# Attention into a gated feed-forward layer: both groups of a head pair multiplied by v in one visit, from the third batch on

## The chip, the cores and the metric

The kernel runs on one core of a Trainium2 chip, as one launch. The metric is the device time of one execution in microseconds (us), as the median of several runs. The core's engines each work through an instruction stream of their own in order: TensorE (PE, with its weight loads shown as PEld), VectorE (DVE), ScalarE (ACT), GpSimd (POOL) and SyncE (SP), which here issues most of the DMAs.

## The reference

Causal attention with a decay that comes from forget gates f, and a feed-forward layer on its output. Batch 8, 8 heads, 576 tokens, head size 64; so 4,608 tokens of width 512, and a hidden width of 1,536.

```python
scores = scale * np.matmul(q, k.transpose(0, 1, 3, 2))
cum = np.cumsum(np.log(np.clip(f, 0.0001, 1.0)), axis=-1)
decay = cum[:, :, :, None] - cum[:, :, None, :]
scores = np.where(causal, -1e9, scores + decay)      # causal: keys after the query
attn = softmax(scores)
x = np.matmul(attn, v)  # to (tokens, heads * head_dim)
out = (silu(x @ w_gate) * (x @ w_val)) @ w_out
```

All inputs and the output are float32; the kernel multiplies in bfloat16 and accumulates in float32.

## The kernel before

**Attention.** The work goes by pairs of heads: 8 batches of 4 pairs, 32 pairs `p`. The two heads of a pair lie side by side on the 128 partitions. Queries are cut into 9 blocks of 64 (block `i` has keys 0 to 64(i+1)), taken in the order 8, 4, 5, 6, 7, 0, 1, 2, 3. For a pair:

- q and k are loaded, made bfloat16 (POOL, from the second batch on) and transposed on PE (`transposes`, line 417) into the one PSUM bank `tt`: first k, six matmuls, copied out by ACT to `kt` (L426); then q, eight matmuls, copied out in two halves to `qz`, each by DVE or ACT (L434). `tt` has one buffer, so each of these uses waits until the copies of the one before have ended.
- for each block the scores are multiplied (L506, bank tag `sp`, two buffers), the mask is added by a second matmul (L510), DVE adds the decay and takes a minimum into `tm` (L523), ACT takes the exponential and its sum (L541), and POOL scales the rows by the reciprocal of the sum into `pk` (L564).
- the weights are transposed, so that keys lie on the partitions: from the second batch on by a DMA transpose that SP issues (`turned`, L586), into `pT1` or `pT0`, two buffers each; in the first batch on PE.
- the transposed weights are multiplied by v (`weighted`, L632), and the sums copied to `xT` by ACT (L642).

The last two steps are done in two groups of blocks, in this order: group 1 is blocks 8 to 4 (19 slots of 128 keys by one block, 10 matmuls), group 0 is blocks 3 to 0 (6 slots, 4 matmuls). A matmul of `weighted` has 64 columns of v as its weights, one head of the pair, and writes 64 partitions; the other head's writes the other 64. All other matmuls in the stretch have 128 weight columns. In the profile these forms are shown as 128*64 and 128*128. Group sums lie in the bank tag `xo`, which has one buffer, so the second group's product waits for the copy of the first one's sums.

**Feed-forward part.** Tokens are cut into 9 tiles of 512. For each, `gate` does 12 times two products with 512 columns (`gp`, `vp`, L674), a tanh on ACT (L680) and two DVE operations (L684, L690); `project` multiplies the result by `w_out` (L721), in four parts, interleaved with the next tile's gates. These products share four PSUM banks (`gv`). A gate product reads `xT` of all four pairs of its batch or batches and so waits for both groups of them. `xT` is a ring of 2,560 tokens.

**The order.** Every step is handed to the class `Planner` with an engine, a priority key (a due time), a length, what it needs, and which buffers it opens and uses. The planner plays the steps against these lengths once, before the program is built: a free engine takes the ready step with the lowest key whose buffers are free. What comes out is the fixed order of each engine's instructions. At run time an instruction waits on semaphores for its inputs and buffers, and all behind it on its engine wait too. `NPS` lists the eight PSUM banks: two for `sp`, one each for `tt` and `xo`, four for `gv`. The key of `weighted` is that of the group's scaling plus `late`, 5.0 from the second batch on; the key of the k transposes of pair `p` is five before the start of its slot (`base(p) - 5`), that of q four before.

Other readers of these steps: `ids["x", p, g]`, the product, gates the cast of v two batches later (`load_v`, which fills one of two buffers); `ids["xT", p, g]` gates the products of the feed-forward part; the DMA transpose of pair p + 2 needs the `pT` buffer that pair p's product frees.

Of the kernel before, what the change touches and what calls it, by code (L numbers as in the profile page):

```python
# [9 lines left out]
F32 = mybir.dt.float32  # L10
# [10 lines left out]
class Planner:  # L21
# [135 lines left out]
def kernel(  # L157
# [11 lines left out]
    nc = tc.nc  # L169
    B, H, S, D = q.shape  # L170
# [3 lines left out]
    P = 128  # L174
    QB = 64
    NB = S // QB
    NPB = H // 2
# [50 lines left out]
    def psum(shape, dt, name, tag):  # L228
        return ps.tile(shape, dt, name=name, tag=tag, bufs=NPS[tag])
# [4 lines left out]
    add = plan.add  # L234
# [16 lines left out]
    xT = consts.tile([P, KD, NRING], BF16)  # L251
# [14 lines left out]
    st = {}  # L266
    ids = {}
# [5 lines left out]
    def base(p):  # L273
        return 10.0 + (SLOT0 * p if p <= NPB else SLOT0 * NPB + SLOT * (p - NPB))
# [115 lines left out]
    def cast_qk(p):  # L390
# [92 lines left out]
    def scores(p):  # L483

        t0 = base(p)
# [6 lines left out]
        for i in ORDER:  # L492
# [4 lines left out]
            key = t0 + width * at / total  # L497
            at += L + 150
            for n, (a, z) in enumerate(parts):
# [13 lines left out]
                def r(i=i, a=a, z=z, n=n, last=last, L=L):  # L513
# [5 lines left out]
                    if n == 0:  # L519
# [8 lines left out]
                m = add("PE", key + 0.02 * n, 0.00042 * (z - a) + (0.03 if last else 0), s, feed,  # L528
                        opens=[("sp", p, i, a)], uses=[("kt", p)])
                ids["s", p, i] = m  # L530
                opens = [("t", p, i)] if n == 0 else []
                if i == ORDER[0] and n == 0:
                    opens.append(("sm", p))
                uses = [("sp", p, i, a), ("cb", p), ("sm", p)] + ([("t", p, i)] if n else [])
                rs = add("DVE", key + 0.3 + 0.02 * n, RED[z - a], r,
                         [m] + ([rs] if n else []), opens=opens,
                         uses=[u for u in uses if u not in opens])

            def x(i=i, L=L):
# [5 lines left out]
                                   uses=[("t", p, i), ("sm", p)])  # L545

        for i0, i1, g in SUMS:
            def rl(i0=i0, i1=i1):
                ls, rl = st["ls", p], st["rl", p]
                nc.vector.tensor_scalar(rl[:, i0:i1], ls[:, i0:i1], 1.0e-9, None, op0=ALU.add)  # L550
                nc.vector.reciprocal(rl[:, i0:i1], rl[:, i0:i1])
            kr = t0 + width * (0.82 if i0 else 1.05)
            a = add("DVE", kr, 0.3, rl, [ids["exp", p, i] for i in range(i0, i1)], uses=[("sm", p)])
            blocks = GROUPS[g]
            ns = []
            for i in sorted(blocks):
                n = blocks.index(i)
                s0 = GOFF[g] + slots_of(g, 0)[0] + n
                m = min(i // 2 + 1, 4)

                todo = [(s0, 0, m)] + ([(GOFF[g], 4, 1)] if i == 8 else [])
                for s0, c, m in todo:
                    def norm(i=i, s0=s0, c=c, m=m, w=len(blocks)):
                        nc.gpsimd.tensor_scalar(  # L564
                            pks[p % 2][:, s0:s0 + w * (m - 1) + 1:w, :],
                            evs[i][:, P * c:P * (c + m)].rearrange("p (c k) -> p c k", k=P),
                            st["rl", p][:, i:i + 1], 1.0, op0=ALU.mult, op1=ALU.mult)
                    needs = [a] + (ids["turn", p - 2, g] if p >= 2 else [])
# [44 lines left out]
    def tiles_of(a, z):  # L613
        return range(max(a, 0) // MT, (z - 1) // MT + 1) if z > 0 else ()

    def weighted(p, g, key):

        b, hp = divmod(p, NPB)
        vt = vts[b % 2]
        blocks = GROUPS[g]  # L620
        w = len(blocks)
        nch = max(blocks) // 2 + 1

        def pv():
            xo = psum([P, 5 * QB], F32, "xo", "xo")
            st["xo"] = xo
            pT = st["pT", p, g].rearrange("p s (h r) -> p s h r", h=2)
            for c in range(nch):
                s0, n = slots_of(g, c)

                for h in range(2):
                    nc.tensor.matmul(xo[64 * h:64 * h + 64, 0:n * QB], vt[:, c, 2 * hp + h, :],  # L632
                                     pT[:, s0:s0 + n, h, :],
                                     start=(c == 0), stop=(c == nch - 1))

        t0 = b * S + GTOK[g][0]

        def ev():
            tok = t0 % NRING
            assert tok + w * QB <= NRING  # L640

            nc.scalar.copy(xT[:, hp, tok:tok + w * QB].rearrange("p (s r) -> p s r", r=QB)[:, ::-1],  # L642
                           st["xo"][:, :w * QB].rearrange("p (s r) -> p s r", r=QB))
        n_slots = GLEN[g]
# [4 lines left out]
        old = [m for t in tiles_of(t0 - NRING, t0 - NRING + w * QB) for m in ids["gv", t]]  # L649
        ids["x", p, g] = a  # L650
        ids["xT", p, g] = add("ACT", key + late, 0.07 + 0.0008 * w * QB, ev, [a] + old,
                              uses=[("xo", p, g)])

# [126 lines left out]
    for b in range(B):  # L780
# [29 lines left out]
    n = KF + (NMT - 1) * (KF + NS)  # L810
# [36 lines left out]
```

## Time and profile before

| | us |
|---|---|
| median of 3 runs (lowest, highest) | 452.73 (452.68, 453.74) |
| the profiled execution's own time | 451.03 |
| its span | 449.3 |
| PE busy in the span | 406.9 (91%) |
| DVE busy | 346.6 (77%) |
| ACT busy | 302.2 (67%) |
| POOL busy | 247.1 (55%) |
| matmuls of the product with v (L632), busy | 34.6, 448 of them |
| copies of its sums to `xT` (L642), busy | 24.9, 64 of them |
| first visit of `weighted` for pair 8, for pair 31 | 126.60, 363.52 |

The profile is of one execution. Busy times of PE include a modelled end of each matmul, since matmuls overlap in the array, so the distance between two starts tells more than the printed length. A wait is put down to what ended it last. Some matmul records (a few in a hundred) are missing from the trace; weight loads are complete. "Visit" below means one run of 128*64 matmuls of `weighted` between other PE work: in the kernel before there are 64 of them, two for each pair. The last product with v ends at about 366 us; behind it come only the feed-forward part of the remaining tiles and the stores.

### The profile page before, as it was taken

How to read it: one execution, taken by the hardware profiler on the slowest of the kernel's cores; microseconds unless marked ns; L12 is line 12 of the kernel's file. 1: busy time of each engine (PE TensorE's matmuls, PEld its weight loads, DVE VectorE, ACT ScalarE, POOL GpSimd, SP SyncE). 2: the span in 40 equal slices, each digit the busy share in tenths (PEclk: the TensorE clock that was granted, in tenths of full speed). 3: DMA queues.
4: the chain of work that ended last, by engine and by line, in shares of the span. 5: the costliest groups of instructions: out<-in, count | busy, mean ns of one | idle time of the engine just before them, and what ended most of it. 6: DMA issues, size and time to landing. Idle time of an engine off the chain costs nothing.

```text
span 449.3 us, 9390 instructions
## 1 busy us (share of the span) xinstructions
PE 406.9 (91%) x2850; PEld 209.1 (47%) x2900; DVE 346.6 (77%) x1071; ACT 302.2 (67%) x838; POOL 247.1 (55%) x441
## 2 busy tenths in 40 slices
PE   1577798998799999999999999999999999999996
PEld 1355553444354554544555554554555444444442
DVE  4877779966899988988998889889989755555542
ACT  4987887745799988987878777777777532322220
POOL 2279989571978887786686777757764400000000
PEclk9998889999899999999999999999999999999999
DMA  8998979999999999999988789988882520101003
GB/s 196 230 187 174 219 153 200 172 220 215 250 221 223 212 242 203 223 224 209 220 223 188 212 217 201 218 182 204 198 138 58 129 74 23 49 24 42 30 23 117
DMA packets 156866, 75.75 MB, mean 169 GB/s; under 512 B 131600, under 2 KB 143376, under 8 KB 156816
## 3 DMA queue, kind: packets, MB, share of 16 engines
q1 hardware_dynamic: 150612, 69.70, 68.3%
q0 software_dynamic: 5808, 4.72, 8.1%
q10 hardware_dynamic: 396, 0.74, 0.6%
q8 instruction: 22, 0.36, 0.3%
q14 instruction: 28, 0.23, 0.2%
HBM read 47.33 MB, written 9.58 MB: 127 GB/s over the span
## 4 chain that ended last, share of the span: by engine, by line
PE 58%; DVE 6%; ACT 4%; issue 2%; DMA 0%; another core or an unknown queue 0%; DVEq 0%; ACTq 0%
PE op L721 17%; PE gp L674 15%; PE vp L674 14%; PE sp L506 6%; PE xo L632 4%; ACT ev L541 2%; DVE t L523 2%; PE tt L417 2%; DVE qz L434 1%; PE sp L510 1%; ACT th L680 1%; DVE ot L730 1%; DVE u L684 1%; ACT qz L434 1%; DVE hh L690 0%
## 5 line engine op out<-in xcount | busy, mean ns | idle before, releaser
L564 POOL TENSOR_SCALAR pk<-ev,rl 128x512 bf16<-128x512 f32 (+3 forms) x320 | 164.1, 533 | 94.2 <-DVE tm L523 34.6
L541 ACT ACTIVATE ev<-t,tm 128x576 f32<-128x576 f32 (+8 forms) x288 | 159.7, 556 | 25.9 <-DVE tm L523 19.0
L523 DVE CUSTOM_DVE_ANT_0 t<-sp,cb 128x512 f32<-128x512 f32 (+7 forms) x288 | 131.6, 475 | 18.5 <-PE sp L510 8.2
L674 PE MATMUL vp<-xT,wv 128*128 128x512 bf16 x413 | 121.4, 379 | 1.8 <-issue 0.6
L721 PE MATMUL op<-wo,hh 128*128 128x512 bf16 x417 | 118.9, 379 | 1.4 <-DVE u L684 0.5
L674 PE MATMUL gp<-xT,wg 128*128 128x512 bf16 x416 | 118.4, 381 | 1.4 <-DVE u L684 0.4
L506 PE MATMUL sp<-kt,qz 128*128 128x512 bf16 (+4 forms) x320 | 88.9, 298 | 17.9 <-DVE tm L523 13.8
L680 ACT ACTIVATE th<-gp 128x512 f32<-128x512 f32 x108 | 63.6, 591 | 57.7 <-PE gp L674 56.8
L684 DVE SCALAR_TENSOR_TENSOR u<-th,gp 128x512 f32<-128x512 f32 x108 | 73.4, 681 | 27.6 <-ACT th L680 27.1
L690 DVE TENSOR_TENSOR hh<-u,vp 128x512 bf16<-128x512 f32 x108 | 73.7, 682 | 12.1 <-PE vp L674 9.5
L510 PE MATMUL sp<-mask,ident 128*128 128x64 bf16 x288 | 55.6, 197 | 0.0
L721 PEld LDWEIGHTS <-hh 128*128 128x128 bf16 x432 | 37.2, 98 | 38.3 <-issue 0.8
L541 ACT ACTIVATION_READ_ACCUMULATOR ev<-t,tm 128x1 f32 x288 | 54.6, 189 | 0.0
L674 PEld LDWEIGHTS <-wg 128*128 128x128 bf16 x432 | 36.5, 98 | 35.1 <-issue 2.0
L674 PEld LDWEIGHTS <-wv 128*128 128x128 bf16 x432 | 36.1, 98 | 33.8 <-issue 1.2
L506 PEld LDWEIGHTS <-qz 128*128 128x128 bf16 x320 | 31.7, 101 | 37.5 <-issue 4.7
L510 PEld LDWEIGHTS <-ident 128*128 128x128 bf16 x288 | 28.5, 99 | 40.0 <-issue 20.5
L632 PE MATMUL xo<-pT,vt 128*64 128x320 bf16 (+4 forms) x448 | 34.6, 271 | 1.2 <-ACT xT L642 1.0
L730 DVE TENSOR_SCALAR ot<-op 128x512 f32<-128x512 f32 x27 | 18.6, 689 | 19.7 <-PE op L721 18.1
L642 ACT CAST xT<-xo 128x320 bf16<-128x320 f32 x64 | 24.9, 389 | 11.3 <-PE xo L632 11.1
L632 PEld LDWEIGHTS <-vt 128*64 128x64 bf16 x448 | 20.5, 110 | 24.9 <-issue 21.3
L401 POOL CAST kb<-kf 96x768 bf16<-96x768 f32 x30 | 25.0, 835 | 11.8 <-ACT qb L395 9.6
(52 smaller groups left out, 300.1 us busy)
## 6 DMA issues: line engine op xcount, KB each, us to landing
kf<-in_k_dram SPq DMA_DIRECT2D x32, 288.0 KB, 4.4
out_dram<-ot SPq DMA_DIRECT2D x36, 256.0 KB, 2.7
qf<-in_q_dram SPq DMA_DIRECT2D x31, 288.0 KB
cb<-cum_f SPq DMA_DIRECT2D x60, 144.0 KB, 4.3
vf<-in_v_dram SPq DMA_DIRECT2D x28, 256.0 KB, 3.3
wg<-in_moe_w_gate_dram POOLq DMA_DIRECT2D x4, 384.0 KB, 6.0
wv<-in_moe_w_val_dram POOLq DMA_DIRECT2D x4, 384.0 KB, 5.4
wo<-in_moe_w_out_dram POOLq DMA_DIRECT2D x3, 512.0 KB, 7.2
```

The source lines that it names most:

```text
L401: copy_by(nc, eng)(st["kb", p], st["kf", p].rearrange("r h c d -> r c h d"))
L506: nc.tensor.matmul(sp[:, :z - a], qz[:, i, :], st["kt", p][:, a:z], start=True, stop=not last)
L510: nc.tensor.matmul(sp[:, z - a - QB:z - a], ident, mask, start=False, stop=True)
L523: nc.vector.tensor_tensor_reduce(out=st["t", p, i][:, a:z], in0=st["sp", p, i, a][:, :z - a], in1=st["cb", p][:, a:z], scale=1.0, scalar=init,
L541: nc.scalar.activation(evs[i][:, :L], st["t", p, i][:, :L], AF.Exp, bias=tm[:, i:i + 1], scale=-1.0, accum_out=ls[:, i:i + 1])
L564: nc.gpsimd.tensor_scalar(pks[p % 2][:, s0:s0 + w * (m - 1) + 1:w, :], evs[i][:, P * c:P * (c + m)].rearrange("p (c k) -> p c k", k=P), st ...
L632: nc.tensor.matmul(xo[64 * h:64 * h + 64, 0:n * QB], vt[:, c, 2 * hp + h, :], pT[:, s0:s0 + n, h, :], start=(c == 0), stop=(c == nch - 1))
L674: nc.tensor.matmul(st[name, t, fc], w_[:, ko, fc * P:(fc + 1) * P], xT[:, ko, x0:x0 + MT], start=(ko == 0), stop=(ko == KD - 1))
L680: nc.scalar.activation(st["th", t, fc], st["gp", t, fc], AF.Tanh, scale=0.5)
L684: nc.vector.scalar_tensor_tensor(st["u", t, fc], st["th", t, fc], 1.0, st["gp", t, fc], op0=ALU.add, op1=ALU.mult)
L690: nc.vector.tensor_mul(st["hh", t][:, fc, :], st["u", t, fc], st["vp", t, fc])
L721: nc.tensor.matmul(st["op", t, s_], st["hh", t][:, fc, s_ * P:(s_ + 1) * P], wo[:, fc, :], start=(fc == 0), stop=(fc == KF - 1))
```

## The change

From pair 8 on (`APART = 2 * NPB`, the third batch) `weighted` is called once for a pair, after both groups have been scaled and their transposes planned. Its one PE step multiplies group 1 into `xo` and directly after it group 0 into a tile with the tag `tt`, the bank of the transposes of q and k. The step opens both banks, needs the transposed weights of both groups, and frees both `pT` buffers at its end. Its key is that of group 0, and its length in the plan is 0.15 plus the columns of both groups, where two steps had 0.15 each. Two copies to `xT` follow on ACT, one for each group, with the later key. Pairs 0 to 7 go as before, one group at a time through `xo`. The sums of `tt` (288 float32 columns) take as many bytes as the transposes there (576 bfloat16).

```diff
+    APART = 2 * NPB
...
             turned(p, g, GLEN[g], ns, kr)
-            weighted(p, g, kr)
+            if p < APART:
+                weighted(p, [g], kr)
+            elif g == SUMS[-1][2]:
+                weighted(p, [s[2] for s in SUMS], kr)
...
-    def weighted(p, g, key):
+    def weighted(p, gs, key):
...
+        bank = dict(zip(gs, ("xo", "tt")))
+        buf = {g: (bank[g], p, "x", g) for g in gs}
 
         def pv():
-            xo = psum([P, 5 * QB], F32, "xo", "xo")
-            st["xo"] = xo
-            pT = st["pT", p, g].rearrange("p s (h r) -> p s h r", h=2)
-            for c in range(nch):
-                s0, n = slots_of(g, c)
-
-                for h in range(2):
-                    nc.tensor.matmul(xo[64 * h:64 * h + 64, 0:n * QB], vt[:, c, 2 * hp + h, :],
-                                     pT[:, s0:s0 + n, h, :],
-                                     start=(c == 0), stop=(c == nch - 1))
...
+            for g in gs:
+                xo = psum([P, S // 2] if bank[g] == "tt" else [P, 5 * QB], F32, "xo", bank[g])
+                st["xo", p, g] = xo
+                pT = st["pT", p, g].rearrange("p s (h r) -> p s h r", h=2)
+                nch = max(GROUPS[g]) // 2 + 1
+                for c in range(nch):
+                    s0, n = slots_of(g, c)
+
+                    for h in range(2):
+                        nc.tensor.matmul(xo[64 * h:64 * h + 64, 0:n * QB], vt[:, c, 2 * hp + h, :],
+                                         pT[:, s0:s0 + n, h, :],
+                                         start=(c == 0), stop=(c == nch - 1))
+
         late = 1.5 if p < EARLY else 5.0
-        a = add("PE", key + late, 0.15 + 0.00042 * QB * n_slots, pv,
-                ids["pT", p, g] + ids["v", b], opens=[("xo", p, g)], uses=[(f"pT{g}", p)])
...
+        a = add("PE", key + late, 0.15 + 0.00042 * QB * sum(GLEN[g] for g in gs), pv,
+                [m for g in gs for m in ids["pT", p, g]] + ids["v", b],
+                opens=[buf[g] for g in gs], uses=[(f"pT{g}", p) for g in gs])
+        for g in gs:
+            w = len(GROUPS[g])
+            t0 = b * S + GTOK[g][0]
+
+            def ev(g=g, w=w, t0=t0):
...
+                nc.scalar.copy(
+                    xT[:, hp, tok:tok + w * QB].rearrange("p (s r) -> p s r", r=QB)[:, ::-1],
+                    st["xo", p, g][:, :w * QB].rearrange("p (s r) -> p s r", r=QB))
...
+            ids["x", p, g] = a
+            ids["xT", p, g] = add("ACT", key + late, 0.07 + 0.0008 * w * QB, ev, [a] + old,
+                                  uses=[buf[g]])
```

More of the change, by code (lines that the diff above doesn't have):

```diff
@@ L614, in tiles_of @@
         return range(max(a, 0) // MT, (z - 1) // MT + 1) if z > 0 else ()
-    def weighted(p, g, key):
+    def weighted(p, gs, key):
         b, hp = divmod(p, NPB)
         vt = vts[b % 2]
-        blocks = GROUPS[g]
-        w = len(blocks)
-        nch = max(blocks) // 2 + 1
+        bank = dict(zip(gs, ("xo", "tt")))
+        buf = {g: (bank[g], p, "x", g) for g in gs}
         def pv():
-            xo = psum([P, 5 * QB], F32, "xo", "xo")
-            st["xo"] = xo
-            pT = st["pT", p, g].rearrange("p s (h r) -> p s h r", h=2)
-            for c in range(nch):
-                s0, n = slots_of(g, c)
-                for h in range(2):
-                    nc.tensor.matmul(xo[64 * h:64 * h + 64, 0:n * QB], vt[:, c, 2 * hp + h, :],
-                                     pT[:, s0:s0 + n, h, :],
-                                     start=(c == 0), stop=(c == nch - 1))
[L636 to L644, printed above, removed]
-        late = 1.5 if p < EARLY else 5.0
-        a = add("PE", key + late, 0.15 + 0.00042 * QB * n_slots, pv,
-                ids["pT", p, g] + ids["v", b], opens=[("xo", p, g)], uses=[(f"pT{g}", p)])
[L649 to L652, printed above, removed]
@@ new lines, in weighted @@
+        late = 1.5 if p < EARLY else 5.0
+        a = add("PE", key + late, 0.15 + 0.00042 * QB * sum(GLEN[g] for g in gs), pv,
[5 more added lines that the diff above has]
+            def ev(g=g, w=w, t0=t0):
+                tok = t0 % NRING
+                assert tok + w * QB <= NRING
+                nc.scalar.copy(
+                    xT[:, hp, tok:tok + w * QB].rearrange("p (s r) -> p s r", r=QB)[:, ::-1],
+                    st["xo", p, g][:, :w * QB].rearrange("p (s r) -> p s r", r=QB))
+            old = [m for t in tiles_of(t0 - NRING, t0 - NRING + w * QB) for m in ids["gv", t]]
+            ids["x", p, g] = a
+            ids["xT", p, g] = add("ACT", key + late, 0.07 + 0.0008 * w * QB, ev, [a] + old,
+                                  uses=[buf[g]])
```

## The prediction

> **What bounds the kernel now.** I read the page's busy lines first, then busy time by stage, then what TensorE (PE) waits for, and last the timeline around the instructions that the change touches. In the table of stages the columns are stretch, length, then busy time and instructions of PE, PE's weight loads, VectorE (DVE), ScalarE (ACT) and GpSimd (POOL), the granted clock, the DMA share and GB/s.
>
> ```profile
> PE 406.9 (91%) x2850; PEld 209.1 (47%) x2900; DVE 346.6 (77%) x1071; ACT 302.2 (67%) x838; POOL 247.1 (55%) x441
> ...
> 0.00:126.00 126.00, 92.83 (x725) 53.65 (x734) 94.00 (x314) 91.41 (x252) 84.25 (x154) 0.95 1.00 202
> 126.00:366.00 240.00, 235.19 (x1768) 119.66 (x1800) 212.33 (x698) 191.10 (x554) 162.85 (x288) 1.00 0.89 194
> 366.00:449.00 83.00, 78.87 (x361) 35.83 (x366) 40.26 (x60) 19.70 (x33) 0.00 (x0) 1.00 0.12 45
> ```
>
> The first visit that the change touches (pair 8) begins at 126.60 us, and the last (pair 31) at 365.1. In that stretch PE is busy 235.19 of 240 us (98%) at a granted clock of 1.00; DVE is next with 212.33 (88%). Before it nothing changes; after it only the feed-forward part (FFN) is left, on PE alone, until the last stores. So the end is PE's own work plus its waits, and PE time saved anywhere after 126 us shortens the tail, because FFN work is always at hand to move up: attention ends at about 366 and PE needs 83 us more.
>
> What PE waits for inside the stretch (microseconds in total, times, longest):
>
> ```profile
> PE sp L506 <- DVE tm L523: 1.0, 4, 0.4
> ...
> PE xo L632 <- ACT xT L642: 0.4, 2, 0.2
> ...
> PE sp L506 <- ACT qz L434: 0.3, 1, 0.3
> ```
>
> All its listed waits come to 2.8 us. Two are of the product with v: the second visit (`xo`) stood until ACT had copied the first one's sums out of the only `xo` bank. No line has the transposes (`tt`) waiting, though one bank holds them.
>
> The price of a visit is in the timeline (start, length, engine, line, operation); the printed length is modelled, so I use distances between starts. This is pair 14, and below it the end of pair 12's first visit:
>
> ```profile
> 185.93 0.59 PE L721 MATMUL op<-wo,hh 128*128 128x512 bf16 x2
> 186.36 0.22 PE L506 MATMUL sp<-kt,qz 128*128 128x128 bf16 x1
> ...
> 186.45 0.60 PE L674 MATMUL vp<-xT,wv 128*128 128x512 bf16 x2
> 186.97 0.36 PE L632 MATMUL xo<-pT,vt 128*64 128x256 bf16 x4
> 187.26 0.26 PE L506 MATMUL sp<-kt,qz 128*128 128x192 bf16 x1
> ```
>
> ```profile
> 164.82 0.20 PE L632 MATMUL xo<-pT,vt 128*64 128x64 bf16 x2
> 164.94 0.39 PE L721 MATMUL op<-wo,hh 128*128 128x512 bf16 x1
> ```
>
> **What the change removes: a visit's entry and exit.** Two 512-column matmuls take 0.43 us when anything of the usual 128*128 form follows (185.93 to 186.36), and 0.52 when a 128*64 product with v follows (186.45 to 186.97): 0.09 us to enter. Leaving costs as much: the last two 64-column matmuls, side by side in the two halves of the array, hold PE 0.12 us until the next start (164.82 to 164.94). At the rate of the 512-column rows (0.215 us each, 0.42 ns a column) they would take 0.03, so leaving costs 0.09. The small visit as a whole lasts 0.29 us (186.97 to 187.26); its 384 columns at 0.42 ns are 0.16, so 0.13 is not streaming: the 0.09 of leaving and about 0.03 on its first pair of matmuls. A visit thus costs 0.22 us beyond its columns, of which 0.19 is certain to go with the switch of form; the 0.03 may stay where the second group begins. The columns themselves stay. The large visit of pair 14 (184.79 to 185.43, 0.64 us for 1,216 columns, 0.51 of streaming) shows the same 0.13, so the excess is per visit and not per matmul.
>
> Pairs 8 to 31 make 24 visits fewer: 24 x 0.19 = 4.6 to 24 x 0.22 = 5.3 us. I take 0.20 each, **-4.8 us**, since the joint itself is not in this trace and the certain part is nearest. All of it lies on PE in the stretch that PE bounds.
>
> **The wait for the one `xo` bank inside a pair.** It goes, as the groups now lie in two banks: **-0.4 us** (the line above), bounds -0.4 and 0.
>
> **What the change adds: a third user of the `tt` bank.** Per pair that bank takes the transposes of k (six matmuls, one ACT copy of 0.63 us), those of q (eight matmuls, two copies of 0.63 and 0.75), and now the small group's sums with an ACT copy of 0.39. A joint visit that starts holds it for about 1.9 us: 0.8 of matmuls, some 0.3 to ACT's start, two copies of 0.39, the large group's first. In all some 4.8 us (1.2 for k, 1.7 for q, 1.9) of the 10.3 us that a pair takes (23 pairs from 126.6 to 363.5), so the bank is not full. But PE is in order, and what waits for the bank stops everything queued behind it on PE: FFN matmuls, then the scores (`sp`) that feed DVE's minimum, ACT's exp and POOL's scaling. To bound this from above I laid the small visits of before against the fills and copies of `tt` as they now stand. In 7 of 24 pairs the bank is still held when the small visit starts, for 0.06 to 1.48 us, 4.4 us together; in 5 the next transposes start within about 2 us after it, and would be held 2.2 us together. So 6.6 us if the order on PE stayed exactly as it is. From below it is zero: the planner writes the order with the bank's occupancy in it and puts FFN pieces (0.43 us each) into the gap. The row nearest to this is the same bank under its two present users: no wait of `tt` on PE in the stretch, and 0.3 us of scores behind a late copy. Its neighbours, late deliveries from DVE and ACT to the scores, are 1.0 + 0.3. I take **+1.2 us**, what those two make together less a little, because the planner avoids known conflicts and misses only those where the real copy is later than planned.
>
> As a page has a rule that speaks against this, it is weighed here. The row is the one above: with two users of the bank PE waited for it zero times in 240 us. The Trainium skill, "Perfetto Trace Analysis", section "Optimizing Tensor Performance", says that independent matmul groups should rotate through different PSUM banks, so that emptying one overlaps the next group's matmuls. Taken strictly, the third user is never hidden and the upper bound holds: -4.8 - 0.4 + 6.6 = +1.4 us. By the row it is -4.0. The row decides for me, since it is this bank under this planner.
>
> **What is moved.** The large group's product waits for the small group's DMA transpose, some 2 us later (184.79 to 186.97). The small group was last before too, so the completion of x moves only by the large group's matmuls ahead of it and one more copy: 0.51 + 0.39, some 0.9 us. Its readers are the gates of the next token tile. At tile 2 they follow closely: its first gate starts at 159.57, and pair 11's last copy at 159.34. There PE has the output projection of tile 1 as cover, which runs from 152 to 203. From tile 3 on gates start 5 us and more after their last visit. Cost 0; without that cover 0.9 once. The DMA transposes (3.4 us each) stay on SP's queue with the same number; their destination buffers (two of each) come free about 2 us later, with the next but one pair some 20 us behind, so nothing queued on SP waits for it. On ACT the large copy moves 2 us back beside the small one; ACT stood 3.6 us before these copies at 5 places in the stretch, and is 80% busy, so a copy more in a row delays an exp by at most 0.39. POOL's cast of the next v waits for the products two batches back, with a whole batch of slack: 0.
>
> **Sum.** -4.8 - 0.4 + 1.2 = -4.0 us. The profiled execution took 451.03 (span 449.3), so 447.0 there. The median of the runs shown, 452.73, stands 1.70 above it; with the same distance the forecast is **448.7 us**.
>
> **Rivals.**
> 1. *The bank of the transposes becomes the limit (slower).* Place: PE's queue, at each joint visit or at the transposes after it. Price: if each pair waits for one ACT copy of 0.39 us, 24 x 0.39 = 9.4, net -4.8 - 0.4 + 9.4 = +4.2, 456.9 us. It decides from a mean wait of 0.22 us per pair (5.2 / 24), that is when somewhat over half of the pairs meet one copy. For it: the 7 and 5 pairs counted above, with 6.6 us if nothing moved (that alone gives 454.1). Against it: a bank half full, no wait on it in the stretch now.
> 2. *The saved PE time is not the end's time (no change).* DVE has 212 of 240 us, over 95% between 120 and 160 us (19.02 and 19.19 of 20). If scores come earlier but DVE does not follow, PE waits for the minimum (`tm`) instead and the 4.8 us come back as longer waits of `sp`: 452.7. Against it: PE's waits on DVE are only 1.0 us in the stretch, and FFN pieces can fill any such hole.
> 3. *The joint order also meets fewer of the other waits.* Of the 2.8 us of listed waits 2.4 are not counted above; without them and without a wait on `tt` -5.3 - 0.4 - 2.4 = -8.1, 444.6. The order after 126 us is made anew, so waits may as well appear; I see no row that says which.
>
> **How the numbers follow.** Forecast (about 447 to 451) 0.65, rival 1 0.18, rival 2 0.12, rival 3 0.05. About 0.3% (1.4 us) is what a measurement of this kernel can tell from no change. Faster: the forecast and rival 3, 0.70; same 0.12; slower 0.18. The range goes from 445.0 (near rival 3's end) up to 455.0, past the upper bound of the bank without a change of order (454.1): it leaves out half of rival 1 and rival 3's end, together under 0.2. The likeliest case alone: -5.7 (all of the gain, no wait) to -1.4, 447.0 to 451.3.
>
> **What the changed profile would show.** Right: 40 visits of form 128*64 in place of 64, from pair 8 on fourteen matmuls in a row; the small group starting within 0.03 us of the streaming rate after the large one; waits of `xo` and `tt` on PE after 126 us under 2 us; attention's last visit earlier or as early, and the tail as dense. Wrong: a line of PE waiting in `xo` for `kt` or `qz`, or in `tt` for `xT`, of 5 us or more (rival 1); waits of `sp` for `tm` grown by several us (rival 2); or a joint that costs as much as an entry, which leaves no gain at all.

## The result

The changed kernel takes 450.87 us (median, 450.51 to 452.27) beside 453.06 us for the kernel before; the ratio is 0.9954 with a 95% interval of 0.9938 to 0.9969, so -2.1 us. A second comparison gave 0.9970 (0.9950 to 0.9989), -1.4 us. The forecast was -4.0 us: the direction holds, about half of the size or more is missing.

### The profile after

First the page's busy lines, then busy time by stretch (stretch, length, busy time and instructions of PE, PE's weight loads, DVE, ACT, POOL, then granted clock, DMA share, GB/s). The profiled execution took 450.51 us, its span is 448.7.

```profile
PE 403.9 (90%) x2851; PEld 209.7 (47%) x2900; DVE 346.8 (77%) x1068; ACT 305.0 (68%) x841; POOL 247.9 (55%) x441
...
126.00:160.00 34.00, 31.72 (x253) 16.78 (x257) 30.91 (x111) 31.55 (x94) 25.81 (x46) 0.97 1.06 217
160.00:366.00 206.00, 202.59 (x1524) 104.79 (x1552) 180.63 (x586) 162.40 (x464) 137.18 (x242) 1.00 0.84 190
```

The same two stretches of the kernel before:

```profile
126.00:160.00 34.00, 32.80 (x269) 16.97 (x272) 32.92 (x117) 31.70 (x95) 25.77 (x47) 1.00 1.08 221
160.00:366.00 206.00, 202.39 (x1500) 102.68 (x1528) 179.41 (x582) 159.41 (x461) 137.08 (x242) 1.00 0.85 190
```

The count behind PE's weight loads tells how far PE got, since each matmul has one load and loads are complete in the trace. From 160 to 366 us the changed kernel does 1,552 in place of 1,528: the same 206 us hold 24 matmuls more. From 126 to 160 us it does 257 in place of 272, 15 fewer, and DVE works 30.91 us in place of 32.92. So the changed kernel gains after 160 us and is behind in its first batch. Part of the latter is the clock: in this stretch the granted clock is 0.97 in place of 1.00, and in this row of the changed kernel, which lies in it, 0.50.

```profile
126.00:128.00 2.00, 2.00 (x15) 1.08 (x14) 1.27 (x6) 1.76 (x5) 2.00 (x5) 0.50 1.85 237
```

PE's waits from 126 to 366 us (total, times, longest), and pair 14's visit in the timeline (start, length, engine, line, operation):

```profile
PE sp L507 <- DVE tm L524: 2.2, 6, 0.6
PE tt L418 <- ACT xT L654: 0.8, 2, 0.5
PE op L730 <- issue: 0.3, 2, 0.2
PE op L730 <- DVE u L693: 0.2, 1, 0.2
```

```profile
183.12 0.59 PE L683 MATMUL vp<-xT,wv 128*128 128x512 bf16 x2
183.64 0.88 PE L638 MATMUL xo<-pT,vt 128*64 128x320 bf16 x14
184.45 0.31 PE L507 MATMUL sp<-kt,qz 128*128 128x320 bf16 x1
```

A joint visit enters at the old price (0.52 for the pair of 512-column matmuls ahead of it, in place of 0.43) and lasts 0.81 us; the two visits of before lasted 0.64 + 0.29 and entered twice. That is 0.81 + 0.09 against 0.93 + 0.18: 0.21 us saved per pair, 5.0 us for 24. The second group joins on without a gap. The bank of the transposes costs PE 0.8 us in two waits, and the `xo` waits are gone.

From 126 to 160 us alone, the wait of scores for DVE's minimum in the kernel before and in the changed one:

```profile
PE sp L506 <- DVE tm L523: 0.3, 1, 0.3
```

```profile
PE sp L507 <- DVE tm L524: 1.6, 5, 0.6
```

The second profiles of both kernels have the same two lines.

**Where the rest went.** To count all PE time in which nothing streams, whatever ended it, I gave each matmul its undisturbed distance of starts from the rows (0.2156 us for 512 columns, 0.029 for 64, linear between; half of it for a 128*64 matmul, as two run side by side), summed it over the weight loads, and took it from the stretch. The time that the array loses at half clock is in this count too; it is taken off by the granted clock of the stretch (1.00, 0.96, 0.97 and 0.95, rounded, in the four profiles from 126 to 160 us, and 1.00 in all after 160). With 0.215 us for each visit taken off as well, waits are left:

| us | not streaming, 126-160 | of it half clock | not streaming, 160-366 | visits | waits, 126-160 | waits, 160-366 |
|---|---|---|---|---|---|---|
| before | 3.8 | 0 | 12.5 | 8, 40 | 2.1 | 3.9 |
| before, second profile | 4.5 | 1.4 | 12.4 | 7, 40 | 1.7 | 3.8 |
| changed | 6.4 | 1.1 | 9.1 | 4, 20 | 4.5 | 4.8 |
| changed, second profile | 6.9 | 1.7 | 9.1 | 4, 20 | 4.3 | 4.8 |

Waits grew by 2.4 to 2.6 us in the third batch and by 1 us after it, 3.3 to 3.6 in all, against 5.2 us of visits (4.9 in the second pair, where one of them falls outside). That leaves a gain of 1.9 us in the first pair of profiles and 1.3 in the second, near the timed 1.4 to 2.1. (With the half clock left in it is 0.8 and 1.0; the profiled executions themselves differ by 0.5 and 1.0 us, 451.03 to 450.51 and 453.27 to 452.27.) What the added waits are for, the list shows in part: 1.3 us of the growth in the third batch is of scores that wait for DVE's minimum. Most of the rest is not in the list.

### The profile page after: what moved, and what is told of

Read it like the earlier page. It is cut to its first block, busy times and chain, and to the rows that moved or that the text cites. A ratio compares the mean times of both kernels' runs of the same rounds, so it can differ in the third digit from the quotient of the medians.

```text
span 448.7 us, 9389 instructions
## 1 busy us (share of the span) xinstructions
PE 403.9 (90%) x2851; PEld 209.7 (47%) x2900; DVE 346.8 (77%) x1068; ACT 305.0 (68%) x841; POOL 247.9 (55%) x441
## 4 chain that ended last, share of the span: by engine, by line
PE 61%; DVE 6%; ACT 4%; issue 2%; DVEq 0%; ACTq 0%
PE op L730 17%; PE gp L683 16%; PE vp L683 15%; PE sp L507 6%; PE xo L638 4%; ACT ev L542 2%; DVE t L524 2%; PE tt L418 2%; DVE u L693 1%; PE sp L511 1%; DVE qz L435 1%; ACT qz L435 1%; DVE hh L699 1%; ACT th L689 1%; DVE ot L739 0%
## 5 line engine op out<-in xcount | busy, mean ns | idle before, releaser
L683 PE MATMUL gp<-xT,wg 128*128 128x512 bf16 x414 | 117.0, 381 | 1.6 <-DVE u L693 0.4
L739 DVE TENSOR_SCALAR ot<-op 128x512 f32<-128x512 f32 x25 | 17.3, 691 | 19.2 <-PE op L730 19.2
L654 ACT CAST xT<-xo 128x320 bf16<-128x320 f32 x64 | 22.9, 397 | 11.9 <-PE xo L638 11.7
L638 PE MATMUL xo<-pT,vt 128*64 128x320 bf16 (+4 forms) x448 | 29.6, 266 | 0.6 <-ACT xT L654 0.6
L398 POOL TENSOR_SCALAR qb<-qf 72x1024 bf16<-72x1024 f32 x28 | 29.2, 1041 | 1.0 <-DMA qf<-in_q_dram 1.0
```

What stands on the lines that cost most here:

```text
L398: eng.tensor_scalar(st["qb", p], qf, -scale, 1.0, op0=ALU.mult, op1=ALU.mult)
L683: nc.tensor.matmul(st[name, t, fc], w_[:, ko, fc * P:(fc + 1) * P], xT[:, ko, x0:x0 + MT], start=(ko == 0), stop=(ko == KD - 1))
```

## The experiments

Three theories of the missing gain. *Stage*: in the third batch DVE is nearly full, a joint visit starves it there, and later pairs keep their gain. *Bank*: the shared bank costs some in every pair. *Order*: the planner's new order of everything else carries the waits. All ratios are to the kernel before, with 95% intervals.

### Again, and by batches

`after2` is the changed kernel unaltered. The other edits, each alone:

```diff
# from16
-    APART = 2 * NPB
+    APART = 4 * NPB
# third
-            if p < APART:
+            if p < APART or p >= APART + NPB:
# switch
+                if bank[g] == "tt":
+                    nc.tensor.matmul(xo[:, 0:QB], ident, mask, start=True, stop=True)
```

> The changed kernel unaltered, for a second profile beside the next three. All theories: ratio to the kernel before 0.993 to 0.998. The stage theory (the gain of 0.22 us per pair is whole where PE bounds the time, and is returned in the third batch, pairs 8 to 11, because DVE is nearly full there): PE time that streams no columns is again over 3 us longer than before between 112 and 160 us, without the visits. The order theory (any new order of the plan moves waits by a few us, anywhere): the same, since the order is the same. If the 3 us were an accident of one execution, they are gone here.

> The joint visit from the fifth batch on alone (pairs 16 to 31); pairs 8 to 15 go as before. Stage theory: 16 pairs keep 0.2 us each and nothing is lost before, so about -3.3 us against the kernel before (ratio 0.993), faster than the changed kernel by 1 us. Bank theory (the shared bank takes back half of the gain in all pairs alike): two thirds of the changed kernel's gain, -1.4 us (0.997). Order theory: anywhere from -4.5 to -0.5 us.

> The joint visit in the third batch alone (pairs 8 to 11); all later pairs as before. Stage theory: slower than the kernel before by 1.5 to 3 us (ratio 1.003 to 1.007): four pairs save 0.9 us and the stage loses some 3.5. Bank theory: a sixth of the gain, -0.3 us, no change to be seen. Order theory: between -2 and +2 us.

> The changed kernel with one matmul of the usual 128*128 form (64 columns, 0.03 us) between the two groups of each joint visit, written where the second group's first product overwrites it; order and plan are the changed kernel's. It puts 24 entries and exits back. If PE bounds the time from pair 8 on and a visit costs 0.19 to 0.22 us: 24 x (0.19 to 0.22 + 0.03) = 5.3 to 6.0 us slower than the changed kernel, so some +3.3 us against the kernel before (1.007). If PE bounds it only from pair 12 on: 4.4 to 5.0 us slower than the changed kernel. If the visit's excess was no part of the end's time: equal to the changed kernel.

| | ratio | interval | us |
|---|---|---|---|
| after2 | 0.9970 | 0.9950 to 0.9989 | -1.4 |
| from16 | 0.9951 | 0.9929 to 0.9972 | -2.2 |
| third | 1.0054 | 1.0032 to 1.0077 | +2.4 |
| switch | 1.0072 | 1.0044 to 1.0100 | +3.3 |

The third batch alone is slower by 2.4 us, as the stage theory had it, and the changed kernel loses there again in its second profile (4.3 us of waits in the table above). The gain of the 16 last pairs is 2.2 us where it wanted 3.3.

`switch` is 4.7 to 5.4 us slower than the changed kernel (+3.3 against -1.4 and -2.1). Its timeline shows what was put back:

```profile
185.76 0.59 PE L685 MATMUL vp<-xT,wv 128*128 128x512 bf16 x2
186.29 0.71 PE L640 MATMUL xo<-pT,vt 128*64 128x320 bf16 x10
186.93 0.20 PE L634 MATMUL xo<-mask,ident 128*128 128x64 bf16 x1
187.06 0.35 PE L640 MATMUL xo<-pT,vt 128*64 128x256 bf16 x4
187.35 0.31 PE L507 MATMUL sp<-kt,qz 128*128 128x320 bf16 x1
```

From 186.29 to 187.35 it is 1.06 us in place of 0.81: one 64-column matmul of the other form in between costs 0.25, of which 0.03 is its own. Without the 24 added matmuls' own 0.7 us, the time rose by 4.0 to 4.7 us, 0.17 to 0.20 for each change of form and back. So the price of a visit is shown in the rows, and most of it in the time. The 4.7 us against `after2`, which was timed beside it, lies in the range for a kernel that PE bounds from pair 12 on (4.4 to 5.0) and below that for one bound from pair 8 on (5.3 to 6.0).

### The order, by the planner's lengths

The planner's own times are part of the kernel: in them PE is idle 5.2 us from 112 to 366 us in the kernel before and 9.9 in the changed one. The next runs vary the length that the planner is told for a visit, or the first joint pair, or share the bank without joining.

```diff
# len18 (first joint pair 8); from12_len18: the same with APART = 12
-        a = add("PE", key + late, 0.15 + 0.00042 * QB * sum(GLEN[g] for g in gs), pv,
+        a = add("PE", key + late, 0.18 + 0.00042 * QB * sum(GLEN[g] for g in gs), pv,
# from12
+    APART = 3 * NPB
# bank: weighted(p, [g], kr) for every group, and
+        bank = {g: "tt" if g == 0 and p >= APART else "xo" for g in gs}
```

> The changed kernel, joint visits from pair 8 on, but the planner is told that a joint visit takes 0.03 us more (0.18 in place of 0.15 plus the columns), which gives a new order and nothing else. In the plan's own time PE is idle 4.05 us between 112 and 165 us in the kernel before, 7.26 in the changed one, 4.65 in this one. Order theory (the third batch's loss is idle time that the planner wrote into the order, by the way the larger step fell): about 2 us faster than the changed kernel, ratio to the kernel before 0.990 to 0.993, and the time without streaming from 126 to 160 us back near that of before less its four visits. Stage theory (a joint visit there starves DVE whatever the order): equal to the changed kernel, 0.995 to 0.997.

> Joint visits from the fourth batch on (pairs 12 to 31). Stage theory: 20 visits less at 0.2 us and no loss in the third batch: -4.0 us, ratio 0.991, faster than the changed kernel and than the one from the fifth batch on. Order theory: the plan has PE idle 5.38 us between 165 and 366 us here, against 1.14 in the kernel before and 2.65 in the changed one, and 1.1 us more before 165, so most of the 4.3 us is given back: -1.5 to 0 us, ratio 0.997 to 1.000, no better than the changed kernel.

> Joint visits from the fourth batch on, with the planner told 0.18 in place of 0.15 us. The plan's idle PE time is 3.06 us between 112 and 165 us (kernel before 4.05) and 3.01 between 165 and 366 (1.14): 0.9 us more than before in all. Order theory: -4.3 + 0.9 = -3.4 us, ratio 0.992, some 2 us faster than the same without the new length. Stage theory: -4.0 us, ratio 0.991, the same as without the new length. A ratio above 0.995 speaks against both.

> The shared bank alone: from pair 8 on two visits a pair as before, but the small group's sums lie in the bank of the transposes. Bank theory (waits for that bank take back half of the gain): 2 to 3 us slower than the kernel before, ratio 1.005 to 1.007, with lines of PE waiting in the product or the transposes for each other's copies of 2 us and more. Order theory: nothing saved, 0.4 us of waits for the other bank gone, 1.6 us more idle PE time in the plan: 0 to +1.5 us, ratio 1.000 to 1.003.

| | ratio | interval | us |
|---|---|---|---|
| len18 | 0.9911 | 0.9886 to 0.9937 | -4.0 |
| from12 | 0.9971 | 0.9946 to 0.9996 | -1.3 |
| from12_len18 | 0.9910 | 0.9883 to 0.9938 | -4.1 |
| bank | 1.0050 | 1.0033 to 1.0066 | +2.3 |

`from12` ends the stage theory: the batch that lost is left alone, and the gain does not come (-1.3 where it wanted -4.0). Its not-streaming time is 3.6 us from 126 to 160, as before, but 11.4 from 160 to 366, of which its 20 visits are 4.3: 7.1 us of waits where the kernel before has 3.9. The waits moved to later pairs.

`len18` hit the order theory's number, but not for its reason. The line that I edited is that of all pairs, so the first eight pairs' visits were told 0.18 as well, which the expectation's "nothing else" leaves out. Its profile has PE at the same amount of work 2 us earlier at 110 us, before any joint visit, and from 126 to 366 us it has 16.8 us without streaming against 15.5 in the changed kernel (14.4 without the half clock). The granted clock is 1.00 from 105 to 133 us in this profile, where the changed kernel's is 0.91 and 0.84 from 119 to 126 and from 126 to 133. So its gain is not shown to be one of the joint visits' order; `early18` below tests that. `from12_len18` came out where both theories had put it, and has the same edit of the first pairs; it decides nothing.

`bank` was slower by more than the order theory had, as much as the bank theory had, but its rows speak against the latter: PE's only waits between the product and the transposes are the last two of these, 0.5 us in all. The first one ends at 125.7 us, before the bank is shared for the first time:

```profile
PE sp L507 <- ACT qz L435: 2.0, 1, 2.0
...
PE xo L635 <- DVE qz L435: 0.3, 1, 0.3
PE xo L635 <- ACT qz L435: 0.2, 1, 0.2
```

### The order alone

```diff
# third30: joint visits for pairs 8 to 11 alone, and their length
-        a = add("PE", key + late, 0.15 + 0.00042 * QB * sum(GLEN[g] for g in gs), pv,
+        a = add("PE", key + late, (0.30 if p >= APART and len(gs) > 1 else 0.15) + 0.00042 * QB * sum(GLEN[g] for g in gs), pv,
# bank24: two visits, small group in the transposes' bank, and their length
+        a = add("PE", key + late, (0.24 if p >= APART else 0.15) + 0.00042 * QB * sum(GLEN[g] for g in gs), pv,
# before21: the kernel before
-        a = add("PE", key + late, 0.15 + 0.00042 * QB * n_slots, pv,
+        a = add("PE", key + late, (0.15 if p < 2 * NPB else 0.21) + 0.00042 * QB * n_slots, pv,
```

> The kernel before, unaltered: a second profile of it, since the first one's execution was faster than nearly all timed runs, and a measure of what the comparison calls no change. All theories: a ratio of 1 within 0.003; PE time without streaming from 126 to 366 us again near 16 us (48 visits of 0.22 and some 6 us of waits).

> Joint visits in the third batch alone, as in the run that was 0.5% slower, but the planner is told 0.30 in place of 0.15 us for them. The plan's idle PE time from 112 to 366 us is 5.8 us here, 10.0 in that run and 5.2 in the kernel before. Order theory: four visits less (-0.9) and +0.6 of planned idle time: -0.3 us, ratio 0.997 to 1.001. Stage theory (a joint visit in that batch starves DVE whatever the order): slower by 1.5 to 3 us again, 1.003 to 1.007.

> Two visits a pair with the small group's sums in the bank of the transposes, as in the run that was 0.5% slower, but the planner is told 0.24 in place of 0.15 us for each visit. The plan's idle PE time from 112 to 366 us is 5.3 us here, 6.8 in that run and 5.2 in the kernel before. Order theory (sharing the bank costs nothing by itself): -0.4 + 0.1 = -0.3 us, ratio 0.998 to 1.001. Bank theory (the sharing costs some 2 us in any order): 1.003 to 1.007.

> The kernel before with nothing changed but the planner's length for a visit from pair 8 on (0.21 in place of 0.15): the same instructions, banks and visits in another order. The plan's idle PE time from 112 to 366 us rises from 5.2 to 6.4 us. Order theory: +1.2 us, ratio 1.001 to 1.004. If the order does not matter: 1.000 within 0.001.

| | ratio | interval | us |
|---|---|---|---|
| before2 | 0.9993 | 0.9967 to 1.0019 | -0.3 |
| third30 | 1.0019 | 0.9997 to 1.0041 | +0.9 |
| bank24 | 0.9990 | 0.9964 to 1.0016 | -0.5 |
| before21 | 1.0045 | 1.0024 to 1.0065 | +2.0 |

`before21` is the kernel before, instruction for instruction, in another order after pair 8, and it is 2.0 us slower; it even exceeds what the plan's idle time gave. So the order by itself moves as much as the change did. `bank24` shares the bank and costs nothing: the 2.3 us of `bank` were its order. `third30` lies between the theories: better than `third` by 1.5 us, and not the gain of 0.9 that four visits are worth. `before2`, the kernel before again, shows no change.

### The same order

If the new order carries the loss, joint visits in the old order should gain in full. Here the planner plans the kernel before; then the first visit of each pair from 8 on is dropped, the joint one is put in the second one's place, after the last copy out of `tt` where that comes later, and both copies to `xT` follow side by side. All other matmuls on PE keep the order of before. (`tag` marks a pair's products and copies from pair 8 on, its third entry is the group, `held` the copies out of `tt` that are still to come.)

```diff
+        for _, n, e in self.order():
+            tag = tags.get(n)
+            if tag and tag[2] == 1:
+                continue
+            if tag and tag[0] == "pv":
...
+                if held:
+                    left = n
+                else:
+                    out.append((n, e))
+                    done = n
+                continue
...
# third_same
+        joint = APART <= p < APART + NPB
# early18, from the kernel before, without joint visits; same_order_early18 is both
-        a = add("PE", key + late, 0.15 + 0.00042 * QB * n_slots, pv,
+        a = add("PE", key + late, (0.18 if p < 2 * NPB else 0.15) + 0.00042 * QB * n_slots, pv,
```

> Joint visits from pair 8 on, but the planner plans the kernel before, and the joint visit is then set where the second visit of a pair stands (after the last copy out of the shared bank, where that is later), with its two copies side by side. On PE all other matmuls stand in exactly the order of before. Order theory: the whole worth of the visits shows, 24 x 0.20 to 0.22 plus 0.4 for the other bank's waits, less under 1 us for the bank: -4.5 to -5.5 us, ratio 0.988 to 0.990; PE time without streaming from 126 to 366 us falls from 16.3 to about 11.5. Joint theory (the joint visits and the shared bank themselves cause the waits): no better than the changed kernel, 0.995 to 0.997.

> The same for the third batch alone (pairs 8 to 11), all else in the order of before. Order theory: four visits less, -0.9 us, ratio 0.997 to 0.999. Joint theory: slower by 1 to 3 us as in the two other runs with joint visits in that batch alone, 1.002 to 1.007.

> The kernel before, with the planner told 0.18 in place of 0.15 us for the visits of pairs 0 to 7 alone; no joint visits. It takes out of the two runs with 0.18 what lay before pair 8: their profiles reached the same amount of PE work 2 us earlier at 112 us. If that is the order of the first pairs: -2 us, ratio 0.994 to 0.997. If the two runs owe their gain to the joint visits' length: 1.000 within 0.002.

> Both: the order of the run before this one, and the joint visits set into it. Order theory: the sum of the two, -6 to -7.5 us, ratio 0.983 to 0.987, the fastest of all. Joint theory: the gain of the order alone and 2 us more, 0.990 to 0.993.

| | ratio | interval | us |
|---|---|---|---|
| same_order | 1.0110 | 1.0071 to 1.0150 | +5.0 |
| third_same | 1.0014 | 0.9989 to 1.0039 | +0.6 |
| early18 | 0.9964 | 0.9935 to 0.9994 | -1.6 |
| same_order_early18 | 1.0091 | 1.0054 to 1.0128 | +4.1 |

The order theory falls in this form. In the old order the joint visits cost 5.0 us where it gave -4.5 to -5.5; the joint theory's "no better than the changed kernel" holds, but not its ratio of 0.995 to 0.997. So the planner's new order, taken over all 24 pairs, is no source of the loss but a repair of part of it. Batch by batch this does not hold: for pairs 8 to 11 alone the old order is the better one, +0.6 us (`third_same`, between the two theories and within noise of none) beside +2.4 (`third`). The loss of `same_order` lies behind 160 us: by the count above its waits are 2.8 us from 126 to 160 (2.1 before) and 12.6 from 160 to 366 (3.9). `same_order_early18`, too, misses both theories. `same_order` from 126 to 366 us, PE's waits and then one pair's case in the timeline:

```profile
PE sp L596 <- DVE tm L613: 5.8, 15, 1.0
PE sp L596 <- ACT qz L524: 1.1, 1, 1.1
PE tt L507 <- ACT kt L516: 0.8, 1, 0.8
PE tt L507 <- ACT xT L736: 0.4, 1, 0.4
```

```profile
199.47 1.10 PE L726 MATMUL xo<-pT,vt 128*64 128x320 bf16 x14
199.54 0.62 ACT L516 COPY kt<-tt 128x576 bf16<-128x576 bf16 x1
200.22 0.76 ACT L736 CAST xT<-xo 128x320 bf16<-128x320 f32 x2
...
201.46 0.42 PE L507 MATMUL tt<-ident,qb 72*128 72x72 bf16 x8
...
201.93 1.05 POOL L487 TENSOR_SCALAR qb<-qf 72x1024 bf16<-72x1024 f32 x1
...
201.96 1.04 DVE L640 TENSOR_SCALAR rl<-ls 128x5 f32<-128x5 f32 x1
...
203.14 0.71 DVE L524 COPY qz<-tt 64x576 bf16<-64x576 bf16 x1
...
203.89 0.63 ACT L524 COPY qz<-tt 64x576 bf16<-64x576 bf16 x1 [1.38 <-DVE qz L524]
...
204.57 0.39 PE L596 MATMUL sp<-kt,qz 128*128 128x512 bf16 x1 [1.15 <-ACT qz L524]
```

Here the shared bank does a small part of what rival 1 feared: the visit's second half waits for the copy of k (0.2 us). The transposes of q come after the two copies to `xT`, but they start right behind two 512-column matmuls and not at a copy's end. q's own copies are late because DVE is: before the first of them it spends 1.04 us on an addition of five columns (the median of these 64 steps is 0.17), while POOL makes the next q bfloat16 from 201.93 to 202.98. So the next pair's first scores wait 1.15 us. Why the addition took so long is not shown; the kernel before has such long ones too.

Listed waits on the bank and on q's copies are 2.3 us in all. The larger part of the list, 5.8 us at 15 places, is of scores for DVE's minimum. Without streaming there are 21.4 us from 126 to 366; without the visits and 1.1 us of half clock some 15 are left, against 6.0 before.

`early18` shows what the two runs with 0.18 owed to the first pairs: -1.6 us without any joint visit. The rest of their gain, some 2.4 us, would be that of the joint visits in that order, little more than the changed kernel's; the intervals of both terms are wider than 1 us to each side.

### Without sharing

```diff
# gv3, from the kernel before
-    NPS = {"sp": 2, "tt": 1, "xo": 1, "gv": 4}
+    NPS = {"sp": 2, "tt": 1, "xo": 1, "gv": 3}
# gv3_same: the order of gv3, joint visits as in same_order (but not held back for tt), but
+    NPS = {"sp": 2, "tt": 1, "xo": 1, "gv": 3, "x2": 1}
+            for g_, bank in ((1, "xo"), (0, "x2")) if joint else ((g, "xo"),):
```

> The kernel before with three PSUM banks in place of four for the feed-forward products and the eighth left empty; a base for the next run. The gates' products wait more often for DVE and ACT: 0 to 10 us slower than the kernel before, ratio 1.000 to 1.022. Both theories say the same.

> The order of the run before this one with joint visits from pair 8 on where the second visits stood, the second group's sums in the empty bank; the bank of the transposes is not shared. Bank theory (the sharing makes the transposes, and behind them the scores, late): 24 x 0.20 to 0.22 and the waits for the one bank saved, nothing lost: 4.5 to 5.5 us faster than gv3. Joint theory (the visit itself delays the scores): equal to gv3 within 1.5 us, or slower.

| | ratio | interval | us |
|---|---|---|---|
| gv3 | 1.0391 | 1.0362 to 1.0420 | +17.7 |
| gv3_same | 1.0516 | 1.0482 to 1.0550 | +23.4 |

`gv3` is slower than its forecast of 0 to 10 us. With a bank of its own the joint visit is still slower, by 5.7 us by the ratios (3.5 in the profiles' spans, 467.7 and 471.2). So sharing the bank is not needed for a loss. PE's waits from 126 to 380 us of `gv3_same`:

```profile
PE sp L596 <- DVE tm L613: 6.9, 19, 1.1
PE vp L770 <- DVE u L780: 3.4, 9, 1.1
PE op L817 <- DVE u L780: 1.9, 6, 0.5
```

and of `gv3`:

```profile
PE sp L506 <- DVE tm L523: 7.2, 17, 1.0
...
PE vp L674 <- DVE u L684: 0.9, 3, 0.4
```

What grew is PE waiting for a `gv` bank that DVE's `u` frees, from 0.9 to 5.3 us in these lines. The wait for the minimum, which grew in `same_order`, did not grow here. With three banks this base has waits that the kernel before does not have, so the pair shows that a joint visit set into an old order loses time without a shared bank, and not how much of the loss with four banks that explains.

### What is settled, and what is open

Settled: a visit costs 0.2 us of PE in the rows, 5 us for 24, and 24 changes of form put back cost 4.0 to 4.7 us of time (`switch`). The joint visits bring back waits of about two thirds of that in the planner's own order (3.3 to 3.6 us), of which the bank itself is 0.8. The order of the other work decides how much is lost: +5.0 us in the old order, -1.4 to -2.1 in the planner's own. Against my theories: it is not the third batch alone (`from12`), not the bank by itself (`bank24`, `gv3_same`), and not the new order by itself (`same_order`).

Open: what the rest of the waits is for, and which property of the joint visit brings them. The list's longest lines have scores waiting for DVE (2.2 us of 3.5 in the changed kernel), so a late DVE is likely, but most of the waits are not in the list. The joint visit puts the large group's product some 2 us later, it keeps PE from scores for 0.8 us in one piece, with two `sp` banks that hold only two scores in advance, and it puts two copies in a row on ACT. No run takes these apart, nor the visit's late place from the visit itself.

Faster than both kernels are `len18` and `from12_len18`, 447.99 and 447.52 us (ratios 0.9911 and 0.9910): the change together with an order of the first pairs that is worth 1.6 us alone.

## Why the prediction was right and wrong

**The visit's price: right.** "-4.8 us" for 24 visits; the rows give 5.0, and `switch` 4.0 to 4.7 in the time, its own matmuls taken off. The 0.03 us that might have stayed at the joint did not stay.

**The wait for the one `xo` bank: right.** No such line is left after 126 us.

**The `tt` bank, "+1.2 us": the step that failed, by its place and its size.** Waits for the bank itself are 0.8 us, within what was given. But I took the bank for the only way in which the joint visit could bring back waits, put every other one at nothing, and sized the term by the row of PE's waits on two users of that bank. What came back were 3.3 to 3.6 us of waits, 2.4 to 2.6 of them from 126 to 160 us, where scores wait for DVE's minimum (1.6 us listed, 0.3 before) and the rest is not in the list. Whether DVE is the cause of all of it stays open. That the row of PE's waits showed 2.8 us before did not say how little a new order would cost. The bound for an unchanged order, 6.6 us of waits for the bank, was too low as well: `same_order` shows some 9 us more of waits than before, and only 2.3 of its listed ones are for the bank or the late q behind it.

**"The planner puts FFN pieces into the gap": half right.** From 160 us on it does (24 matmuls more in the same stretch). In the third batch it does not; there PE waits 0.6 us longer per pair.

**Costs put at nothing.** The completion of x: right at tile 2, whose first gate starts at 160.19 in place of 159.57. SP's queue and POOL's cast: no wait of PE on them after 126 us in the list.

**The rivals.** Rival 1 (the bank becomes the limit) had the sign of what happens in the old order, but the bank is a small part of the listed waits there too. Rival 2 (saved time returns as waits for `tm`) is nearest to what happened: I had its place, 120 to 160 us with DVE over 95% full, and weighed it at 0.12 because listed waits were 1.0 us. Its listed row grew to 2.2 only; of some 9 us of waits in the stretch the list shows 3.5. Rival 3 named the new order and said that no row tells its sign; `before21` shows that the order alone is worth 2 us.

**The profile's signs.** 40 visits, fourteen matmuls in a row, no loss at the joint, `xo` and `tt` waits under 2 us and an earlier last visit (364.1, the small one stood at 365.1) all came as written, while the time did not follow: these signs watched the joint. The one sign for DVE, waits of `sp` for `tm` grown by several us, looked at the list, where they grew by 1.2.

## What to carry to other kernels

Price a saved switch of PE's form from distances of starts: the forecast of 4.8 us met 5.0 in the rows, and 4.0 to 4.7 in the time when the switches were put back. Then ask what the joined work does to the engine next in line: here, with PE 98% full and DVE 88 to 97%, about two thirds of the saving came back as waits. Where a planner writes the order, every change of a step is also a new order: reorder the unchanged kernel by a harmless constant first, to see how much of a result is luck (here -1.6 to +2.0 us). Count the work done in a stretch, for example by weight loads, rather than the waits listed in it, and look at the granted clock of the stretch before putting a loss down to the change.

## What the runs showed of the hardware

**Price of a change of form.** Between 128*128 and 128*64 matmuls PE loses 0.09 us on the way in and 0.10 on the way out, in all visits alike; two groups of 128*64 into different banks follow each other with no loss. The Trainium skill, "TensorEngine Tiling (Array Packing)", section "Key Properties", says that a change of tiling mode drains TensorE, and that a change of tile alone does not; it gives no time. The rows agree, with 0.2 us for there and back.

**The granted clock falls at different places.** These rows hold the drop of the kernel before's first profile, and then of the changed kernel's:

```profile
112.00:118.00 6.00, 5.25 (x34) 2.66 (x34) 4.45 (x20) 4.44 (x16) 5.39 (x11) 0.72 0.90 262
```

```profile
124.00:130.00 6.00, 5.78 (x38) 3.12 (x38) 4.60 (x15) 5.15 (x14) 5.51 (x10) 0.72 1.13 204
```

The clock is 0.50 from 126 to 128 us in the row shown further up, so 0.72 over 6 us is about 3.4 us at half speed, some 1.7 us of full work. In the second profile of the kernel before it falls in both places (0.75 and 0.72). The Trainium skill, "TensorE: Matmul & The Clock Gate", Part 1, has a free-running activity window of about 3.4 us, which is idle before the slow state; the length of the falls fits that, but no wait as long as that stands just before them. At 122 to 126 us it stood for q's copies of pair 10: 1.42 us in the first profile of the kernel before, where no fall followed, 1.48 in the second and 2.06 in the changed kernel, where one followed 0.4 and 1.0 us after the end of the wait. Up to the first visit of pair 8, PE has the same order in both kernels, so the place of the fall is not shown to be the change's doing.

The time goes with it from run to run. Of the 29 runs of the kernel before beside `after2`, the five at a mean granted clock of 0.984 took 450.4 to 451.2 us, the seven at 0.987 and 0.988 451.8 to 452.6, and the eleven at 0.972 to 0.974 453.3 to 455.0; so the mean alone does not tell it, and the place of the falls, which only profiles show, may matter.
